# Dividing the loads of an attention and expert kernel into pieces, issued at two marks of every step

## The chip, the cores and the metric

The kernel runs on one core of one Trainium2 chip. The metric is device time in microseconds (us) of one execution. An execution is measured several times, and the median is compared. The profile comes from one execution that the hardware profiler recorded, with a time of its own.

Engines in the text: TensorE (PE in profile lines; PEld is its weight loads), VectorE (DVE), ScalarE (ACT), GpSimd (POOL) and SyncE (SP), which only issues transfers. GpSimd issues transfers as well, and those that change the number type go through it. Every engine works through its own instructions in order, and waits on semaphores for others.

## The reference

Sliding-window attention with a few sink positions, and then a sparse layer that only 128 tokens of each batch pass through. Shapes are 4 batches, 8 heads, 768 positions, 64 values to a head; the window is 128 wide and the first 4 positions are sinks.

```python
scores = 1 / sqrt(D) * q @ k.T                    # per batch and head, 768 x 768
keep = (pos[None, :] < 4) | ((rel >= 0) & (rel < 128))      # rel = query - key
a = softmax(where(keep, scores, -1e9))
x = (a @ v) laid out as [batch, position, 8 * 64]
s = x @ w_gate                                    # one score per token
top = the 128 tokens of each batch with the largest s
out = x
out[top] = x[top] + sigmoid(s[top]) * (relu(x[top] @ w1) @ w2)
```

w1 is 512 x 1024 and w2 is 1024 x 512, all inputs are float32.

## The kernel before

The attention is cut into 24 steps. A step is (b, g, jp): batch b, group g of four heads (0 or 1), and a pair jp of query blocks of 128 positions (0, 1, 2). The loop at line 455 runs over them with n from 0 to 23; s = 3g + jp counts the six steps of a batch. The order of instructions on each engine is the order in which the code is written, since the scheduling is manual.

Within a step, TensorE computes the scores of the next step (`scores`, line 214), ScalarE takes their exponentials (line 255) into `PT`, and TensorE multiplies those by the values (`values`, line 259, once for t = 0 and once for t = 1, two heads each). VectorE then divides by the row sums (lines 275 and 276) into X. Query and key come in as 128-position rows with several heads beside each other, and `transposes` (line 187) turns them: K of the coming group after the values of jp = 0, Q before the values of jp = 1. VectorE and ScalarE copy the results out of PSUM.

Half a block of queries (64 rows) sees one whole block of 128 keys, one half block and the sinks. So each matmul over values reads one of three tiles: `vb` holds the values as loaded, a whole block of 128 keys; `vE` holds the lower 64 rows of a block and below them the sink values; `vF` holds sink values and the upper 64 rows. `half_values` (line 115) copies those halves out of `vb`, on GpSimd after the first steps, in pieces of two blocks for all four heads; `sink_values` (line 111) loads the sink rows with two small transfers on SP. There are two `vb` buffers, each for a batch with all eight heads, and two of `vE` and `vF`, one for each group.

Loads are issued like this:

- K and Q, with a change from float32 to bfloat16, by GpSimd (`load_qk`, line 84). One load brings four heads, 384 KB as the profile counts it. The loads of a group of batch b + 1 are issued in the first two steps of the same group of batch b.
- The first group's K and Q in eight loads (`load_qk_first`, line 92), and then K and Q of the second group directly behind them.
- Values by SP: the first six blocks one by one (line 107), the second group of batch 0 in one load (line 165 and above), and then two heads at a time (`load_v`, line 102), at s = 0, 1, 2 and 4.
- w1 and w2 by GpSimd in two loads each, at s = 0 and 2, and at s = 3 and 5 of batch 1 (lines 512 to 517).
- The finished rows are stored by SP, two blocks in one transfer, at the end of each step of g = 1 (`finish_rows`, line 289).

SP's and GpSimd's transfers each use eight semaphores in turn, so a transfer also waits for the eighth before it on its queue.

The sparse layer of a batch runs beside the attention of the next batch (`m` in the loop: `spread`, `count`, `columns`, `ranks`, `choose`, `index`, `gather`) and of the one after that (`mm`: `pick`, `up`, `down`, `scatter`). The last batch's sparse layer follows the loop (lines 547 to 570).

Two small functions in the opening, `first_values` (line 158) and `late_loads` (line 163), set buffers to constants and issue loads; `late_consts` and `late_consts2` make index tables.

## Time and profile before

| what | us |
|---|---|
| median of 3 runs | 153.49 (151.84 to 153.93) |
| the profiled execution | 154.2 |
| its span, first to last instruction | 152.4 |
| mean granted TensorE clock | 0.939 of full speed |

The busy time of each engine over the span, with its number of instructions, is this:

```profile
PE 114.7 (75%) x2888; PEld 96.2 (63%) x2888; DVE 99.3 (65%) x306; ACT 69.8 (46%) x92; POOL 61.6 (40%) x99
```

The transfers are these (queue, packets, MB, and the time of the packets as a share of 16 transfer engines over the span). Queue 0 holds what GpSimd issues, queue 1 what SP issues:

```profile
q0 software_dynamic: 7200, 10.49, 38.7%
q1 hardware_dynamic: 28868, 13.28, 33.9%
```

And this is the granted TensorE clock in 40 slices of the span, in tenths:

```profile
PEclk9998699969999997899599999999999999999985
```

Shares of busy time are means over the whole span, and they hide that the loop ends at some 131 us and that a tail of some 20 us without bulk loads follows. The last value loads are issued at 94.72 us, and the last step's division ends at 131.6 us. Idle time of one engine costs nothing unless another waits for it, so the waits have to be read beside the busy time. A wait is put down to what came last by the profile; "issue" is a wait for nothing that the profile shows.

### The profile page before, as it was taken

To read this page: it belongs to the slowest core of one execution; us is meant where nothing else is said; L and a number is where in the kernel's file an instruction comes from. 1 tells how busy PE (TensorE), PEld (TensorE's weight loads), DVE (VectorE), ACT (ScalarE), POOL (GpSimd) and SP (SyncE) were. 2 spreads that over 40 slices of the span, in tenths; PEclk is the share of its full clock that TensorE was granted. 3 is DMA by queue.
4 is the path that set the end of the run, shared out by engine and by line. 5 is a ranking of instruction groups with operands and counts; after the bars stand their busy time and mean duration, and the time that the engine had idled before them with its cause. 6 is when DMAs were issued, how large, how long until landed. Compare 5 with 4: busy or idle time off the path is not lost. (4 is left out here: it accounts for less than half of the span.)

```text
span 152.4 us, 6554 instructions
## 1 busy us (share of the span) xinstructions
PE 114.7 (75%) x2888; PEld 96.2 (63%) x2888; DVE 99.3 (65%) x306; ACT 69.8 (46%) x92; POOL 61.6 (40%) x99
## 2 busy tenths in 40 slices
PE   6846996389599575983986959799897988886700
PEld 2325886289489366873876848669696975746600
DVE  5726787239569971693675945967799958956220
ACT  3084454525568341552564608517755673250200
POOL 7947879085097000960594018414610021102220
PEclk9998699969999997899599999999999999999985
DMA  2799999999979999699999983973300044411201
GB/s 37 107 168 173 252 247 228 235 141 217 263 244 141 207 206 223 162 174 240 321 191 201 205 187 28 269 268 133 94 4 4 4 164 187 156 55 69 73 2 69
DMA packets 36098, 24.19 MB, mean 159 GB/s; under 512 B 25829, under 2 KB 31845, under 8 KB 36069
## 3 DMA queue, kind: packets, MB, share of 16 engines
q0 software_dynamic: 7200, 10.49, 38.7%
q1 hardware_dynamic: 28868, 13.28, 33.9%
q8 instruction: 23, 0.38, 1.0%
q14 instruction: 7, 0.05, 0.1%
HBM read 24.41 MB, written 7.34 MB: 208 GB/s over the span
## 5 line engine op out<-in xcount | busy, mean ns | idle before, releaser
L255 ACT ACTIVATE pt<-sc 128x1024 f32<-128x1024 f32 (+1 forms) x48 | 43.5, 951 | 25.8 <-PE sc L250 25.5
L270 PE MATMUL xg<-vb,pt 128*64 128x65 f32 x704 | 50.7, 233 | 5.8 <-issue 5.8
L270 PE MATMUL xg<-vE,pt 128*64 128x65 f32 x384 | 47.0, 235 | 8.5 <-issue 4.3
L270 PEld LDWEIGHTS xg<-vb,pt 128*64 128x64 f32 x704 | 46.1, 146 | 6.3 <-issue 6.3
L270 PEld LDWEIGHTS xg<-vE,pt 128*64 128x64 f32 x384 | 37.7, 147 | 11.9 <-issue 10.0
L270 PE MATMUL xg<-vF,pt 128*64 128x65 f32 x320 | 41.2, 229 | 0.0
L270 PEld LDWEIGHTS xg<-vF,pt 128*64 128x64 f32 x320 | 33.1, 145 | 0.0
L117 POOL COPY vE<-vb 64x512 f32<-64x512 f32 (+1 forms) x27 | 15.7, 587 | 36.1 <-DMA vb<-in_v_dram 29.6
L275 DVE RECIPROCAL rz<-xg 128x4 f32<-128x4 f32 x48 | 8.6, 179 | 28.6 <-PE xg L270 28.3
L276 DVE TENSOR_TENSOR x<-xg,rz 128x256 f32<-128x256 f32 x48 | 20.4, 424 | 1.7
L118 POOL COPY vF<-vb 64x512 f32<-64x512 f32 x21 | 14.2, 677 | 15.2 <-PE sc L250 6.4
L226 PE MATMUL sc<-QT,KT 64*64 64x192 bf16 (+2 forms) x384 | 17.1, 251 | 3.3 <-issue 1.9
L286 DVE CUSTOM_DVE_ANT_0 junk<-x,wgb 128x512 f32<-128x512 f32 (+1 forms) x30 | 18.8, 661 | 0.3
L336 DVE TENSOR_SCALAR_CACHE_REDUCE G<-sbc,scol 128x512 bf16<-128x512 f32 (+5 forms) x26 | 15.4, 637 | 0.4 <-ACT sbc L318 0.3
L232 PE MATMUL sc<-band,ident_b 64*64 64x256 bf16 x192 | 14.2, 282 | 0.0
L226 PEld LDWEIGHTS <-KT 64*64 64x64 bf16 x384 | 8.1, 110 | 6.8 <-issue 3.6
L245 PE MATMUL sc<-QT,ksk 64*64 64x128 bf16 (+1 forms) x96 | 10.5, 214 | 1.3 <-issue 1.3
L434 POOL DMA_INDIRECT out_dram<-yo,idx x4 | 4.1, 1018 | 18.0 <-DVE yo L430 17.2
L207 ACT COPY KT<-trp 128x768 bf16<-128x768 bf16 x7 | 5.7, 809 | 12.2 <-PE trp L197 12.2
L250 PE MATMUL sc<-QT,ksk 64*64 64x128 bf16 x96 | 10.9, 225 | 0.0
L375 POOL DMA_INDIRECT xe<-out_dram,idx x4 | 4.2, 1054 | 15.8 <-issue 12.2
L197 PE MATMUL trp<-ident_b,kb 128*64 128x128 bf16 x192 | 8.7, 241 | 1.1 <-DMA kb<-in_k_dram 1.0
(96 smaller groups left out, 185.7 us busy)
## 6 DMA issues: line engine op xcount, KB each, us to landing
out_dram<-x SPq DMA_DIRECT2D x12, 512.0 KB
vb<-in_v_dram SPq DMA_DIRECT2D x12, 384.0 KB
kb<-in_k_dram POOLq DMA_DIRECT2D x7, 384.0 KB, 7.8
qb<-in_q_dram POOLq DMA_DIRECT2D x7, 384.0 KB, 9.4
w_sb<-in_moe_w_dram POOLq DMA_DIRECT2D x4, 512.0 KB, 7.8
vb<-in_v_dram SPq DMA_DIRECT2D x6, 128.0 KB
vb<-in_v_dram SPq DMA_DIRECT2D x1, 768.0 KB
kb<-in_k_dram POOLq DMA_DIRECT2D x4, 96.0 KB, 3.5
```

The costliest lines, as they stand in the source:

```text
L117: e.tensor_copy(out=vE[g][0:64, c0:c1, :, 0:D], in_=src[0:64])
L118: f.tensor_copy(out=vF[g][64:128, c0:c1, :, 0:D], in_=src[64:128])
L197: PE.transpose(out=trp[64 * l:64 * l + 64, i, :], in_=src[:, l, half * (CT // 2) + i, :], identity=ident_b[:])
L226: PE.matmul(out=sc[e][64 * h:64 * h + 64, l, i, 64 * h:64 * h + n], lhsT=kt[r, e, q0:q0 + 64], rhs=qt[r, e, q0:q0 + n], start=(i == 0), st ...
L232: PE.matmul(out=sc[e][64 * h:64 * h + 64, l, :, :].rearrange("p k (a x n) -> p k a x n", a=2, x=2)[:, :, :, h, :], lhsT=ident_b[r, r], rhs ...
L245: PE.matmul(out=sc[e][0:64, l, 0:n, 192:256], lhsT=ksk[g][r, e, :], rhs=(qt[r, e, q0 - 64:q0 - 64 + 256].rearrange("p (k c) -> p k c", k=2 ...
L250: PE.matmul(out=sc[e][64:128, l, 0:2, 0:64], lhsT=ksk[g][r, e, :], rhs=qs, start=False, stop=True, skip_group_check=True)
L255: ACTE.activation(out=pt[:, :, :, :].rearrange("p l k c -> p l (k c)")[:, :, 0:n], in_=sc[e][:, :, :, :].rearrange("p l k c -> p l (k c)") ...
L270: PE.matmul(out=xg[64 * m:64 * m + 64, i, l, :], lhsT=PT[(b, g, kc // 2, t)][:, l, kc % 2, off:off + 64], rhs=val, start=first[m], stop=(i ...
L276: DVE.tensor_tensor(out=X[b][:, js[0]:js[0] + 2, 256 * g:256 * g + 256].rearrange("p j (l e d) -> p j l e d", l=2, e=2)[:, :, :, t, :], in ...
L286: DVE.tensor_tensor_reduce(out=junk[:, c0:c1], in0=X[b][:, j, c0:c1], in1=wgb[:, c0:c1], scale=1.0, scalar=0.0, op0=ALU.mult, op1=ALU.add, ...
L336: DVE.tensor_scalar(out=self.G[c][:, lo:z], in0=self.sbc[:, lo:z], scalar1=SCOL[self.b][:, c:c + 1], scalar2=0.0, op0=ALU.is_gt, op1=ALU.a ...
```

## The change

`load_qk` now loads one pair of heads of K or Q, `load_v` one head, and `load_w` a quarter of w1 or w2. Before most of these loads, `gate` writes one element of the destination on VectorE. The load overwrites that element, so it has to wait until VectorE has come to the gate. The gates are at two marks of a step: after the division for t = 0, and at the step's end.

The value buffers hold four heads each and there are three of them, used in turn by the groups; the row pitch of a block in them (`VS`) is 128 elements and not 96. `half_values` now copies one head with all its blocks, and leaves out the vF copy of the last block, which no matmul reads. The second group's Q and values of batch 0 are loaded from step 0's first mark on. Values of the coming groups are loaded from jp = 2 of the group two before to jp = 0 of the group before, K and Q over the three steps of the group two before. The eight weight pieces go out at the ends of steps 5 to 8 and 11 to 14. Rows are stored one block at a time by `store_rows`, ahead of the sink loads.

```diff
@@ -23,7 +23,7 @@
 FF = 1024
 NSINK = 4
 VW = D + 1
-VS = 96
+VS = 128
 CT = 12
 
 
@@ -61,7 +61,7 @@
     def const(shape, dt, name):
         return cp.tile(shape, dt, name=name, tag=name)
 
-    vb = [const([128, H, NB, VS], FP32, f"vb{i}") for i in range(2)]
+    vb = [const([128, 4, NB, VS], FP32, f"vb{i}") for i in range(3)]
     vE = [const([128, NB, 4, VW], FP32, f"vE{i}") for i in range(2)]
     vF = [const([128, NB, 4, VW], FP32, f"vF{i}") for i in range(2)]
     vsk = const([NSINK, 2 * B, 4, VW], FP32, "vsk")
@@ -81,13 +81,19 @@
 
     QK, KT, QT, PT, X, SCOL = {}, {}, {}, {}, {}, {}
 
-    def load_qk(b, g, ts=(0, 1)):
-        for t in ts:
-            dst = stg.tile([128, 2, CT, D], BF16, name=("kb", "qb")[t], tag=("kb", "qb")[t])
-            QK.setdefault((b, g), [None, None])[t] = dst
-            POOL.dma_start(
-                out=dst[:, :, :, :].rearrange("p l c d -> p l (c d)"),
-                in_=(k, q)[t][b, 4 * g:4 * g + 4, :, :].rearrange("(l e) (p c) d -> (e p) l (c d)", e=2, c=CT))
+    def gate(ap):
+        DVE.memset(ap, 0.0)
+
+    def load_qk(b, g, t, l, gated=True):
+        if l == 0:
+            QK.setdefault((b, g), [None, None])[t] = stg.tile([128, 2, CT, D], BF16, name=("kb", "qb")[t],
+                                                              tag=("kb", "qb")[t])
+        dst = QK[(b, g)][t]
+        if gated:
+            gate(dst[0:1, l, 0, 0:1])
+        h = 4 * g + 2 * l
+        POOL.dma_start(out=dst[:, l, :, :].rearrange("p c d -> p (c d)"),
+                       in_=(k, q)[t][b, h:h + 2, :, :].rearrange("e (p c) d -> (e p) (c d)", c=CT))
 
     def load_qk_first(half):
         if half == 0:
@@ -99,9 +105,10 @@
                     in_=src[0, 0:4, 384 * half:384 * half + 384, :].rearrange(
                         "(l e) (p c) d -> e p l (c d)", e=2, c=6)[e])
 
-    def load_v(b, h0, h1):
-        SP.dma_start(out=vb[b % 2][:, h0:h1, :, 0:D].rearrange("p h c d -> p (h c) d"),
-                     in_=v[b, h0:h1, :, :].rearrange("h (c p) d -> p (h c) d", p=128))
+    def load_v(b, g, hh):
+        buf = vb[(2 * b + g) % 3]
+        gate(buf[0:1, hh, 0, 0:1])
+        SP.dma_start(out=buf[:, hh, :, 0:D], in_=v[b, 4 * g + hh, :, :].rearrange("(c p) d -> p c d", p=128))
 
     def load_v_block(c):
         SP.dma_start(out=vb[0][:, 0:4, c, 0:D],
@@ -112,10 +119,21 @@
         SP.dma_start(out=vE[g][64:64 + NSINK, :, :, :].rearrange("s c h o -> s c (h o)"), in_=src)
         SP.dma_start(out=vF[g][0:NSINK, :, :, :].rearrange("s c h o -> s c (h o)"), in_=src)
 
-    def half_values(b, g, c0, c1, e, f):
-        src = vb[b % 2][:, 4 * g:4 * g + 4, c0:c1, 0:D].rearrange("p h c d -> p c h d")
-        e.tensor_copy(out=vE[g][0:64, c0:c1, :, 0:D], in_=src[0:64])
-        f.tensor_copy(out=vF[g][64:128, c0:c1, :, 0:D], in_=src[64:128])
+    def half_values(b, g, c0, c1, h0, h1, e, f):
+        src = vb[(2 * b + g) % 3][:, h0:h1, c0:c1, 0:D].rearrange("p h c d -> p c h d")
+        e.tensor_copy(out=vE[g][0:64, c0:c1, h0:h1, 0:D], in_=src[0:64])
+        if c0 < NB - 1:
+            c1 = min(c1, NB - 1)
+            f.tensor_copy(out=vF[g][64:128, c0:c1, h0:h1, 0:D], in_=src[64:128, 0:c1 - c0])
+
+    def load_w(i):
+        if i < 4:
+            gate(w1_sb[0:1, i, 0:1])
+            POOL.dma_start(out=w1_sb[:, i, :], in_=moe_w1.rearrange("(dc p) f -> p dc f", p=128)[:, i, :])
+        else:
+            r = slice(2 * i - 8, 2 * i - 6)
+            gate(w2_sb[0:1, 2 * i - 8, 0:1])
+            POOL.dma_start(out=w2_sb[:, r, :], in_=moe_w2.rearrange("(fc p) d -> p fc d", p=128)[:, r, :])
 
     def fill(times):
         f = w_ps.tile([128, 512], FP32, name="fill", tag="w")
@@ -135,7 +153,8 @@
         POOL.affine_select(out=r[:, 1, :], in_=r[:, 1, :], compare_op=ALU.is_ge, fill=-1e9, base=-1,
                            pattern=[[-1, 64]], channel_multiplier=1)
     load_qk_first(1)
-    load_qk(0, 1)
+    for l in range(2):
+        load_qk(0, 1, 0, l, gated=False)
     DVE.memset(vsk[:, :, :, D:VW], 1.0)
     SP.dma_start(out=vsk[:, :, :, 0:D].rearrange("s (b g) h d -> s (b g h) d", b=B),
                  in_=v[:, :, 0:NSINK, :].rearrange("b h s d -> s (b h) d"))
@@ -161,7 +180,6 @@
             load_v_block(c)
 
     def late_loads():
-        load_v(0, 4, 8)
         SP.dma_start(out=wgb[:], in_=moe_w_gate.partition_broadcast(128))
         POOL.memset(vE[1][64:128, :, :, :], 0.0)
         POOL.memset(vF[1][0:64, :, :, :], 0.0)
@@ -169,6 +187,7 @@
         POOL.memset(vF[1][64:128, :, :, D:VW], 1.0)
         POOL.memset(ksk[1][:], 0.0)
         DVE.memset(vb[1][:, :, :, D:VW], 1.0)
+        DVE.memset(vb[2][:, :, :, D:VW], 1.0)
         DVE.memset(ones_b[:], 1.0)
 
     iotas = []
@@ -262,7 +281,7 @@
         for i, j in enumerate(js):
             for l in range(2):
                 hh = 2 * l + t
-                whole = vb[b % 2][:, 4 * g + hh, :, 0:VW]
+                whole = vb[(2 * b + g) % 3][:, hh, :, 0:VW]
                 terms = [(0, j, 0, vE[g][:, j, hh, :]), (1, j, 64, whole[:, j, :])]
                 if j > 0:
                     terms += [(0, j - 1, 128, whole[:, j - 1, :]), (1, j - 1, 192, vF[g][:, j - 1, hh, :])]
@@ -286,11 +305,13 @@
             DVE.tensor_tensor_reduce(out=junk[:, c0:c1], in0=X[b][:, j, c0:c1], in1=wgb[:, c0:c1], scale=1.0,
                                      scalar=0.0, op0=ALU.mult, op1=ALU.add, accum_out=acc[:, j:j + 1])
 
+    def store_rows(b, js):
+        for j in js:
+            SP.dma_start(out=out[b, j * 128:(j + 1) * 128, :], in_=X[b][:, j, :])
+
     def finish_rows(b, js):
         if js[0] == 0:
             SCOL[b] = sp.tile([128, NB], FP32, name="scol", tag="scol")
-        SP.dma_start(out=out[b, js[0] * 128:(js[-1] + 1) * 128, :].rearrange("(j p) d -> p j d", p=128),
-                     in_=X[b][:, js[0]:js[-1] + 1, :])
         if b < B - 1:
             dots(b, js, 0, DM, SCOL[b])
             return
@@ -448,7 +469,7 @@
     for t in range(2):
         transposes(0, 0, t, (1,))
     for c in range(2):
-        half_values(0, 0, c, c + 1, POOL, DVE)
+        half_values(0, 0, c, c + 1, 0, 4, POOL, DVE)
     late_loads()
 
     moe = {}
@@ -457,6 +478,7 @@
         js = [2 * jp, 2 * jp + 1]
         last = b == B - 1
         nxt = (b, 1) if g == 0 else (b + 1, 0)
+        far = (b + 1, g)
         m, mm = moe.get(b - 1), moe.get(b - 2)
         if n + 1 < len(steps):
             nb, ng, njp = steps[n + 1]
@@ -478,43 +500,52 @@
                 if m and s == 0:
                     m.spread(0, NB)
                     m.gates_exp()
+                if nxt[0] < B:
+                    if n == 0:
+                        for l in range(2):
+                            load_qk(0, 1, 1, l)
+                        load_v(*nxt, 0)
+                        load_v(*nxt, 1)
+                    if jp == 0:
+                        load_v(*nxt, 2)
+                if far[0] < B:
+                    if jp > 0:
+                        load_qk(*far, jp - 1, 1)
+                    if jp == 2:
+                        load_v(*far, 0)
         if last and s == 4:
             moe[b].count((0, 1))
         if m and s == 3:
             m.index()
         if nxt[0] < B and jp == 0:
             transposes(nxt[0], nxt[1], 0)
-        if b + 1 < B:
-            if s == 0:
-                X[b + 1] = xp.tile([128, NB, DM], FP32, name="x", tag="x")
-            if s in (0, 1, 2, 4):
-                h = 2 * (0, 1, 2, 0, 3)[s]
-                load_v(b + 1, h, h + 2)
-            if s in (0, 1):
-                load_qk(b + 1, 0, (s,))
-            if s in (3, 4):
-                load_qk(b + 1, 1, (s - 3,))
+        if b + 1 < B and s == 0:
+            X[b + 1] = xp.tile([128, NB, DM], FP32, name="x", tag="x")
+        if g == 1:
+            store_rows(b, js)
+        if nxt[0] < B:
+            if jp == 0:
+                sink_values(*nxt)
+                load_v(*nxt, 3)
+        if far[0] < B:
+            if jp < 2:
+                load_qk(*far, jp, 0)
+            else:
+                load_v(*far, 1)
+        if 5 <= n < 9:
+            load_w(n - 5)
+        if 11 <= n < 15:
+            load_w(n - 7)
+        if n < 2:
+            for c in range(2 * n + 2, 2 * n + 4):
+                half_values(0, 0, c, c + 1, 0, 4, POOL, DVE)
+        if nxt[0] < B:
+            for hh in ((), (0, 1), (2, 3))[jp] if n < 3 else ((0,), (1, 2), (3,))[jp]:
+                half_values(*nxt, 0, NB, hh, hh + 1, POOL, POOL)
         if n == 0:
             late_consts()
         if n == 1:
             late_consts2()
-        if nxt[0] < B:
-            if jp == 0:
-                sink_values(*nxt)
-            if n > 2:
-                half_values(*nxt, 2 * jp, 2 * jp + 2, POOL, POOL)
-            elif n == 2:
-                for c in (0, 2, 4):
-                    half_values(*nxt, c, c + 2, POOL, POOL)
-        if n < 2:
-            for c in range(2 * n + 2, 2 * n + 4):
-                half_values(0, 0, c, c + 1, POOL, DVE)
-        if b == 1 and s in (0, 2):
-            r = slice(s, s + 2)
-            POOL.dma_start(out=w1_sb[:, r, :], in_=moe_w1.rearrange("(dc p) f -> p dc f", p=128)[:, r, :])
-        if b == 1 and s in (3, 5):
-            r = slice(2 * (s - 3), 2 * (s - 3) + 4)
-            POOL.dma_start(out=w2_sb[:, r, :], in_=moe_w2.rearrange("(fc p) d -> p fc d", p=128)[:, r, :])
         if last and g == 0:
             dots(b, js, 0, 256, PART)
         if g == 1:
```

## The prediction

> **What bounds the kernel now.** I read the page first, then the waits of TensorE, then the timeline around its longest idle times, then tables by stretches of time. Two rows of the page's 40 slices (3.81 us each) set the question:
>
> ```profile
> PE   6846996389599575983986959799897988886700
> DMA  2799999999979999699999983973300044411201
> ```
>
> While the DMA row stands at 9 (8 to 87 us), TensorE falls to 5 and 3 again and again; once the DMA row is at 3 and 0 (103 us on), TensorE stays at 8 and 9. ScalarE and GpSimd are far from full. The waits of TensorE from 14 to 108 us (engine, line, what it waited for, us in all, times, longest) are these:
>
> ```profile
> PE xg L270 <- issue: 10.1, 6, 2.4
> PE xg L270 <- DMA vE<-vsk: 4.2, 2, 2.6
> PE sc L226 <- issue: 1.9, 2, 1.6
> PE sc L245 <- issue: 1.3, 1, 1.3
> ```
>
> "issue" means that nothing the profile shows was waited for. Where such a wait falls is the clue (the timeline of TensorE: start, us, line, operation, count, idle time before):
>
> ```profile
> 50.50 0.24 PE L226 MATMUL sc<-QT,KT 64*64 64x192 bf16 x1
> 52.36 0.36 PE L226 MATMUL sc<-QT,KT 64*64 64x192 bf16 x7 [1.62 <-issue]
> ```
>
> One of eight equal score matmuls runs, 1.62 us pass, and the other seven follow. All eight read the same KT and QT and write one tile, so no data can be missing. Long waits end at 24.08, 31.06, 42.01, 52.36, 58.79, 71.09, 83.20, 89.51 and 99.24 us; they took 1.32, 1.41, 1.88, 1.62, 2.65, 2.42, 1.30, 1.84 and 1.25 us, 15.7 us together. I counted TensorE's instructions between neighbours in a table by stretches (from, to, length, then busy us and count of PE, PEld, DVE, ACT, POOL, then the granted clock, the DMA share and GB/s):
>
> ```profile
> 30.00:40.50 10.50, 9.07 (x255) 8.31 (x255) 7.37 (x20) 4.96 (x6) 5.32 (x8) 0.84 1.01 200
> 51.00:57.00 6.00, 3.78 (x126) 3.33 (x125) 4.98 (x19) 2.91 (x4) 0.00 (x0) 1.00 1.15 207
> 57.00:70.00 13.00, 9.39 (x255) 8.65 (x255) 7.68 (x21) 5.82 (x7) 6.00 (x8) 0.87 0.95 191
> ```
>
> Matmuls plus weight loads are 510, 251, 510; the other five stretches give 259, 509, 507, 254, 508. That is 256 or twice 256 every time. The page has a queue for instructions:
>
> ```profile
> q8 instruction: 23, 0.38, 1.0%
> ```
>
> That is 23 packets of 16.5 KB; the 2 x 2888 matmuls and weight loads of the whole run are 22.6 times 256. So I read these nine waits as TensorE's program arriving late, behind the bulk loads: between 108 and 152 us, with a mean DMA share of 0.20, the list of TensorE's waits names no "issue". The 2.65 us at 58.79 is named a DMA of sink values, but falls on the same count and its issue lies 14 us back. Only the wait at 28.66 (1.53 us, same name) stands off the count; it is a sink load behind a 768 KB and a 384 KB value load on SP.
>
> The Trainium skill ("Runtime: NRT & Kernel Launch", "Instruction fetch mechanics") says that blocks of 256 instructions are fetched while the present one runs and are mostly hidden, with room for 2,048 on TensorE. By that rule the nine waits would not be fetches, and this change would have only the 1.53 us to win, and the sum below would come to 156.6 us. The row with seven of eight matmuls speaks against the rule here.
>
> **The change, part by part.** The sum is made against the profiled execution: 154.2 us, of which the span is 152.4. The median of the three runs is 153.49, so 0.7 comes off at the end. The bytes stay the same.
>
> *Smaller pieces, spread out.* A group's K or Q load of 384 KB becomes two of 192, a value load of 384 KB becomes two of one head (192 KB), a weight load of 512 KB two of 256. The issue lines of the page give the length of what a fetch stands behind (count, KB, median us to landing):
>
> ```profile
> kb<-in_k_dram POOLq DMA_DIRECT2D x7, 384.0 KB, 7.8
> qb<-in_q_dram POOLq DMA_DIRECT2D x7, 384.0 KB, 9.4
> kb<-in_k_dram POOLq DMA_DIRECT2D x4, 96.0 KB, 3.5
> qb<-in_q_dram POOLq DMA_DIRECT2D x4, 96.0 KB, 4.1
> ```
>
> On a straight line between these, 192 KB lands in about 5 to 6 us, some 3 us sooner; the longest wait is 2.65, so all 15.7 us could go. Against that stands the ceiling: from 14.3 to 107.9 us the DMA share is 0.98 of 93.6 us, 91.7 us of work, and the highest share held over 7 us is 1.17 (22.6 to 30.0). That work needs 91.7/1.17 = 78.4 us, so at most 15.2 us can be saved, and a loop that gets faster loads the queues as before. Bounds 0 and 15.2; I take two thirds of 15.7, **-10.5**.
>
> *The sink wait.* Three value pieces (576 KB) instead of the loads named above now precede that sink load: **-1.5**, bounds 0 and 1.5.
>
> *The clock.* After such waits the granted clock is 0.78 (32.4 to 37.8 us), 0.78 (54.9 to 61.7) and 0.66 (72.5 to 77.3): 5.4x0.22 + 6.8x0.22 + 4.8x0.34 = 4.3 us at the most. In the first of these VectorE is busy 4.69 of 5.4 us and would hold the step anyway. **-1.5**, bounds 0 and 4.3.
>
> *The start.* Q of group (0,1) was issued at 8.59 us; now it waits for a mark after the first normalising (VectorE, 16.51 + 0.42 = 16.9), two issues of 0.72 follow, and it lands 3.5 to 6 us later, at 22 to 24. Its transposes stand ahead of step 1's values on TensorE, which now reaches them near 19.5: 2 to 4.5 us lost. In return the first K and Q halves, for which TensorE waits 0.46 and 1.91 us at 9.72 and 12.15, no longer share the engines with it or with 768 KB of values. Bounds -0.4 and +4.5; **+2.0**.
>
> *The gates.* 62 one-element memsets on VectorE; the nearest rows are 65 and 72 ns (one-partition memsets, lines 153 and 159): 4.3 us of VectorE. What queues behind each is the normalising that frees TensorE's xg. A gate's own wait (earlier readers and loads of that buffer) is over steps before. VectorE is near full only in the steps that copy transposes (4.69 of 5.4, 4.61 of 4.7, 5.17 of 5.7 us), a third of all: **+1.4**, bounds 0 and 4.3.
>
> *GpSimd.* 18 more load issues at 0.72 = 13 us, copies 28 pairs of 384 and 320 columns instead of 21 pairs of 512. By the uncontended rows (0.39 us for 256 columns, 0.60 for 512) a pair is 0.49 + 0.44, 26 us against 25.5. GpSimd goes from 61.6 to about 75 busy us, well under the span. Each issue now waits for VectorE's mark, and the value copies, gathers and scatters stand behind it. This bites where a weight piece comes before head 3's copies at the end of a group (steps 5, 8, 11, 14): normalising 0.65, gate 0.1, issue 0.72, copies 0.93 and some 0.2 of signals make 2.6 us, while TensorE comes to head 3 after the next scores and half the values, 0.95 + 0.95. 4 x 0.6 = 2.4 at most; **+1.2**.
>
> *SP.* 27 more issues of about 0.4 us, on a queue that mostly waits. A store or sink load behind a gated load now waits for a mark as well; sinks are still issued over two steps before use. Nothing added, and up to 1.5 us per group if a sink is late. Leaving out the last block's unused vF copy and the new row pitch of the value tile: nothing; both lie on GpSimd or in transfers, and are in the pairs counted above.
>
> Sum: 154.2 - 10.5 - 1.5 - 1.5 + 2.0 + 1.4 + 1.2 = 145.3, less 0.7: **144.6 us**.
>
> Shares above 1 in the stretches shown say that several loads are in flight at once, so the number of loads (45 more) costs their issue and no more. A rule against all this is in the Trainium skill, "DMA: Bandwidth & Descriptors", "Bandwidth" and "Anatomy of one DMA": transfers should be 1 MiB or more, and each has about 2 us of fixed cost. By it, as an estimate, 45 x 2 = 90 us if they ran one by one, for some 235 us.
>
> **The rivals.** *The waits stay (no change).* If a fetch stands behind all that is queued and not behind one load, the same bytes at a share near 1 delay it as before. For it: the shares of stretches with waits are 0.94 to 1.17 whatever was loading. With half the 15.7 us kept: 154.2 - 7.8 + 4.6 = 151.0, less 0.7 = 150.3; with all kept, 158.8 - 0.7 = 158. I put its centre at 152.
>
> *The marks make Q late (slower).* Q's last piece is issued half-way through a group's third step and is transposed before the values of the next group's second step: 1.5 steps, 6.6 us at 4.4 us a step. Landing above that stops TensorE once per group. At 9.4 us (the median of the large Q loads) it costs 2.8 x 7 = 19.6 us: 164 us. It decides from a landing of about 7.9, where 1.3 x 7 eats the gain of 8.9. Against it: the small loads land in 4.1, at shares of about 0.8 to 1.08, however.
>
> *The pieces are not pieces:* no; the changed program issues each load by itself.
>
> **How the numbers follow.** About 2% (3.1 us) is what a measurement of this kernel can tell from no change. The forecast has 0.70, the first rival 0.17, the late Q 0.13. The forecast's best case is the ceiling, 154.2 - 15.2 - 0.7 = 138.3. The range runs from 139 to 156, with 0.06 below and 0.13 above. Faster 0.70, same 0.17, slower 0.13.
>
> **What would show it.** Right: waits for "issue" on TensorE from 14 to 108 us fall from 13 to 3 or 5 us; steps 3 to 17 (26.4 to 104.5 us now, 5.2 us each) take 4.4 to 4.7; the DMA share there goes above 1.05; a new wait for Q near 20 us. Wrong: issue waits still on multiples of 256 and near 10 us (first rival); waits of TensorE for qb in most groups (second); GpSimd's copies in front of TensorE's waits for vE (my 1.2 too small).

## The result, and the profile after

The changed kernel is slower: 161.69 us (160.02 to 161.78, four runs) against 153.71 (151.84 to 154.72, four runs) of the kernel before beside it. The ratio is 1.054, with a 95% interval of 1.041 to 1.066. The profiled execution took 161.74 us, its span 159.8, and the mean granted clock was 0.901 (0.939 before). Here and below a median is over all executions, and a ratio compares the faster executions of a kernel (within 1.5% of its fastest) with those of the kernel before in the same session.

First the rows of the page's 40 slices (now 4.0 us each):

```profile
PE   6846906699978694998149996799499887895900
POOL 7922870393773672078315590465336010202220
PEclk9995675899999999699956999999879999999995
DMA  3899496279899999789975799989950025331110
```

TensorE stands still in the sixth slice (20 to 24 us), and the clock in the slices after it is 0.5 to 0.8. The DMA row now has gaps at 16 to 20 and at 24 to 32 us, where before it stood at 9: loads are held back just before and just after TensorE's wait, and while it waits (20 to 24) the row is at 9. The waits of TensorE from 14 to 115 us (line, what it waited for, us in all, times, longest) say what took the place of the old ones:

```profile
PE xg L289 <- POOL vF L127: 5.6, 3, 3.3
PE trp L216 <- DMA qb<-in_q_dram: 5.1, 2, 4.8
PE xg L289 <- issue: 4.6, 3, 2.5
PE xg L289 <- POOL vE L124: 3.6, 3, 1.9
PE trp L216 <- issue: 1.5, 1, 1.5
PE sc L245 <- issue: 1.3, 1, 1.3
PE sc L251 <- issue: 0.8, 1, 0.8
```

The four "issue" rows make 8.2 us. Before they made 13.3, and 15.9 with the 2.65 us that the list names a DMA of sinks. The sink row is gone. New are 5.1 us for Q, once, and 9.2 us for the two copies that GpSimd makes.

Where this falls is seen when a fixed event of every step is compared: the first division of step n (VectorE's reciprocal, from its timeline), in us.

| step n | before | after | after minus before |
|---|---|---|---|
| 2 | 25.46 | 33.30 | +7.84 |
| 11 | 71.58 | 71.60 | +0.02 |
| 13 | 81.60 | 88.34 | +6.74 |
| 15 | 92.91 | 96.11 | +3.20 |
| 19 | 113.42 | 120.85 | +7.43 |
| 23 | 129.75 | 137.44 | +7.69 |

So the start loses 7.8 us, steps 2 to 11 win 7.8 (somewhat over half of the gain that was expected), and from there to step 19 another 7.4 are lost. From the first division of step 12 to that of step 13 the change takes 7.55 us longer (88.34 - 74.64 against 81.60 - 75.45), of which 3.5 come back by step 15, and at step 18 2.8 us longer (120.85 - 111.02 against 113.42 - 106.40). In both GpSimd has issued a gather shortly before. Little changes after that.

**The start.** GpSimd's timeline (start, us, line, operation, count, idle time before):

```profile
15.90 1.39 POOL L184 MEMSET vE<- 64x1560 f32 x1
17.35 1.39 POOL L185 MEMSET vF<- 64x1560 f32 x1
...
19.55 1.07 POOL L95 DMA_DIRECT2D qb<-in_q_dram  x2 [0.28 <-DVE x L295]
```

The mark itself was set at 17.97 us. The Q loads of group (0,1) still had to stand behind some 3.3 us of GpSimd's own constants (`late_loads`), which ran to 19.26, 1.3 us past the mark. TensorE's timeline shows the bill:

```profile
24.96 0.28 PE L216 MATMUL trp<-ident_b,qb 128*64 128x128 bf16 x1 [4.81 <-DMA qb<-in_q_dram]
25.52 1.46 PE L216 MATMUL trp<-ident_b,qb 128*64 128x128 bf16 x23 [0.28 <-DMA qb<-in_q_dram]
```

And then the clock (a table by stretches: from, to, length, busy us and count of PE, PEld, DVE, ACT, POOL, granted clock, DMA share, GB/s):

```profile
25.50:29.70 4.20, 4.18 (x87) 4.20 (x87) 1.73 (x5) 0.81 (x1) 0.00 (x0) 0.57 0.22 46
```

At a clock of 0.57 the values of step 1 take longer than they would at full speed, so the wait costs more than its own length. Of the 7.8 us, 1.1 come from step 0 (its first division at 17.39 instead of 16.30; in the other versions it lies between 15.82 and 17.65). From there to step 2, TensorE waits 6.5 us (5.1 for Q, 1.4 for a copy) instead of 1.6. The other 1.8 fit the clock, 4.2 us at 0.57, but no run shows that part by itself. The DMA share is 0.22 there and GpSimd idle, since its next load waits for a mark as well:

```profile
29.71 0.54 POOL L95 DMA_DIRECT2D kb<-in_k_dram  x1 [6.47 <-DVE kb L85]
```

**The gathers.** GpSimd's timeline around the first gather, after:

```profile
74.45 1.19 POOL L396 DMA_INDIRECT xe<-out_dram,idx  x1 [0.28 <-POOL vF L127]
77.01 0.50 POOL L124 COPY vE<-vb 64x384 f32<-64x384 f32 x1
81.19 0.45 POOL L127 COPY vF<-vb 64x320 f32<-64x320 f32 x1 [3.68 <-DMA xe<-out_dram,idx]
```

and TensorE behind it:

```profile
77.56 0.27 PE L289 MATMUL xg<-vE,pt 128*64 128x65 f32 x1 [1.94 <-POOL vE L124]
...
81.69 0.37 PE L289 MATMUL xg<-vF,pt 128*64 128x65 f32 x1 [3.33 <-POOL vF L127]
```

The vF copy that follows a gather on GpSimd waits in this program until the gather has landed, and this copy is of head 3 of the group that TensorE has already begun. In the kernel before the same dependence is there, and TensorE's list names no copy. The rows are the first gather there; the last one, from GpSimd's list of waits, shows the dependence at the second:

```profile
65.72 1.20 POOL L375 DMA_INDIRECT xe<-out_dram,idx  x1 [0.28 <-POOL vF L118]
66.96 0.60 POOL L117 COPY vE<-vb 64x512 f32<-64x512 f32 x1
73.94 1.02 POOL L118 COPY vF<-vb 64x512 f32<-64x512 f32 x1 [6.38 <-PE sc L250]
...
POOL vF L118 <- DMA xe<-out_dram,idx: 5.0, 1, 5.0
```

Before, the gather goes out 1.1 us ahead of the first division of step 10 (66.85), after the change 5.4 us behind it (69.08). Of the 9.2 us for copies, 7.6 lie in steps 12 and 18. And the copies by pairs of blocks were needed one step after another, those by heads are all needed in the group's first step. (The version without marks, below, has the copies by heads too, and TensorE waits for none of them.)

### The profile page after: what moved, and what is told of

It reads as the page before. It is cut to its first block, busy times and chain, and to the rows that moved or that the text cites. A ratio compares the mean times of both kernels' runs of the same rounds, so it can differ in the third digit from the quotient of the medians.

```text
span 159.8 us, 6749 instructions
## 1 busy us (share of the span) xinstructions
PE 118.5 (74%) x2885; PEld 99.1 (62%) x2888; DVE 95.1 (60%) x368; ACT 69.8 (44%) x92; POOL 70.2 (44%) x131
## 5 line engine op out<-in xcount | busy, mean ns | idle before, releaser
L289 PE MATMUL xg<-vb,pt 128*64 128x65 f32 x704 | 50.0, 231 | 0.0
L95 POOL DMA_DIRECT2D kb<-in_k_dram x14 | 7.6, 548 | 32.7 <-PE trp L216 14.2
L124 POOL COPY vE<-vb 64x384 f32<-64x384 f32 (+1 forms) x34 | 17.7, 527 | 7.3 <-DMA vb<-in_v_dram 5.9
L127 POOL COPY vF<-vb 64x320 f32<-64x320 f32 x28 | 13.5, 484 | 11.0 <-DMA xe<-out_dram,idx 7.1
L305 DVE CUSTOM_DVE_ANT_0 junk<-x,wgb 128x512 f32<-128x512 f32 (+1 forms) x30 | 17.1, 606 | 0.3
L251 PE MATMUL sc<-band,ident_b 64*64 64x256 bf16 x192 | 14.7, 285 | 0.8 <-issue 0.8
L216 PE MATMUL trp<-ident_b,qb 128*64 128x128 bf16 x192 | 9.0, 248 | 7.6 <-DMA qb<-in_q_dram 7.5
L226 ACT COPY KT<-trp 128x768 bf16<-128x768 bf16 x7 | 5.7, 809 | 19.2 <-PE trp L216 19.2
L216 PEld LDWEIGHTS <-qb 128*64 128x64 bf16 x192 | 7.4, 127 | 9.3 <-issue 8.6
L216 PE MATMUL trp<-ident_b,kb 128*64 128x128 bf16 x192 | 9.9, 259 | 2.1 <-issue 1.5
L455 POOL DMA_INDIRECT out_dram<-yo,idx x4 | 4.0, 1007 | 16.2 <-DVE yo L451 15.9
```

The source lines that it names most:

```text
L95: POOL.dma_start(out=dst[:, l, :, :].rearrange("p c d -> p (c d)"), in_=(k, q)[t][b, h:h + 2, :, :].rearrange("e (p c) d -> (e p) (c d)", ...
L124: e.tensor_copy(out=vE[g][0:64, c0:c1, h0:h1, 0:D], in_=src[0:64])
L127: f.tensor_copy(out=vF[g][64:128, c0:c1, h0:h1, 0:D], in_=src[64:128, 0:c1 - c0])
L216: PE.transpose(out=trp[64 * l:64 * l + 64, i, :], in_=src[:, l, half * (CT // 2) + i, :], identity=ident_b[:])
L251: PE.matmul(out=sc[e][64 * h:64 * h + 64, l, :, :].rearrange("p k (a x n) -> p k a x n", a=2, x=2)[:, :, :, h, :], lhsT=ident_b[r, r], rhs ...
L289: PE.matmul(out=xg[64 * m:64 * m + 64, i, l, :], lhsT=PT[(b, g, kc // 2, t)][:, l, kc % 2, off:off + 64], rhs=val, start=first[m], stop=(i ...
```

## The experiments

Each edit is to the changed kernel unless it says otherwise. "Issue" sums below are from the list of TensorE's waits from 14 to 115 us, each from a single profile. In the order in which they stand here, the first four come from one session, the next three from a second, the next four from a third and the last from a fourth. The kernel before had medians of 154.13, 153.16, 152.76 and 153.62 us in them, so a difference of medians across sessions is uncertain by a us or more, and the ratios, each to the kernel before of the same session, are given too.

**Q of (0,1) back in the opening.**

```diff
-    for l in range(2):
-        load_qk(0, 1, 0, l, gated=False)
+    for t in range(2):
+        for l in range(2):
+            load_qk(0, 1, t, l, gated=False)
...
                     if n == 0:
-                        for l in range(2):
-                            load_qk(0, 1, 1, l)
                         load_v(*nxt, 0)
```

> The changed kernel with one part undone: Q of group (0,1) is issued without a gate, directly behind K of that group, as before the change. Theory A (the opening's late Q costs what step 1 lost): TensorE's wait for qb near 20 us (4.81 us) is gone, step 1's first division comes at about 22 to 24 us instead of 28.75, and the time falls by 4 to 6 us to about 156 to 157.5. Rival (the wait moves to the next late thing, as the DMA engines are free from 26 to 31 us anyway): step 3 comes as late as before, and the time stays within 1.5 us of 161.7.

Measured: 153.49 us (152.25 to 156.47, ten runs), ratio to before 0.996 [0.991, 1.001]. Two load issues moved back, without their marks, take 8.2 us off, nearly the whole loss, and more than was expected. The rest of the list stays:

```profile
PE xg L290 <- POOL vF L127: 3.8, 2, 2.8
PE xg L290 <- issue: 3.7, 6, 1.2
PE xg L290 <- POOL vE L124: 2.5, 3, 1.5
```

**The copies of heads 1 to 3 one step earlier, ahead of the gather.**

```diff
-            for hh in ((), (0, 1), (2, 3))[jp] if n < 3 else ((0,), (1, 2), (3,))[jp]:
+            for hh in ((), (0, 1), (2, 3))[jp] if n < 3 else ((0,), (1, 2, 3), ())[jp]:
```

> The changed kernel with the copies of heads 1, 2 and 3 all at the end of a group's second step (before the gather), none at the end of the third. Theory B (head 3's copies stand behind the gather on GpSimd, and its vF copy waits for the gather's landing): TensorE's waits for vE and vF (9.2 us in the changed kernel) fall to under 3, steps 12 and 18 no longer lose 4.9 and 2.5 us, and the time falls by 5 to 8 us to 154 to 157. Rival (GpSimd is simply late with everything): the waits for vE and vF stay over 6 us and the time stays within 1.5 us of 161.7.

> Both edits together. If A and B are separate losses, they add: 161.7 - 5 - 6.5, about 149 to 152, faster than the kernel before. If one hides the other: 154 to 157.

Measured: alone 162.22 us (158.51 to 164.17), ratio 1.056 [1.045, 1.067]; together with the early Q 155.13 (149.39 to 158.18), not told apart from before and inside the range named for losses of which one hides the other. Alone the waits for the copies fell to 1.7 us, but the wait moved. In the first of the two:

```profile
PE xt L414 <- DMA xe<-out_dram,idx: 6.6, 2, 4.5
PE trp L216 <- DMA qb<-in_q_dram: 5.6, 3, 3.0
PE xg L289 <- issue: 5.3, 4, 1.7
PE xg L289 <- POOL vE L124: 1.7, 2, 1.4
```

TensorE's transposes of the gathered rows (`xt`) now wait for the gather itself. So not the order of copy and gather is the fault: GpSimd comes to both too late.

**The kernel before with the same pieces** (K, Q, value, weight loads and stores cut as in the change; no marks, no third buffer, the old places):

```diff
-            POOL.dma_start(
-                out=dst[:, :, :, :].rearrange("p l c d -> p l (c d)"),
-                in_=(k, q)[t][b, 4 * g:4 * g + 4, :, :].rearrange("(l e) (p c) d -> (e p) l (c d)", e=2, c=CT))
+            for l in range(2):
+                h = 4 * g + 2 * l
+                POOL.dma_start(out=dst[:, l, :, :].rearrange("p c d -> p (c d)"),
+                               in_=(k, q)[t][b, h:h + 2, :, :].rearrange("e (p c) d -> (e p) (c d)", c=CT))
```

> The kernel before with every load and store divided into the same pieces, all issued at the places of before, without gates, buffers by batch as before. Theory C (a fetch of TensorE's instructions stands behind what is queued altogether, so only spreading helps): issue waits on multiples of 256 instructions stay at 12 to 16 us in all, time within 2 us of 153.5. Rival (it stands behind the one load in front of it, as the prediction had it): they fall to under 8 us and the time falls to 145 to 149.

Measured: 156.01 us (150.76 to 159.25), not told apart from before. The waits that the pieces should have shortened are still there:

```profile
PE xg L271 <- issue: 8.8, 5, 2.7
PE sc L227 <- issue: 2.7, 1, 2.7
```

All "issue" rows make 11.8 us (13.3 before). The size of a load is at most a small part of what these waits depend on.

**The gather earlier** (early Q, and the gather given out before the values of a batch's fifth step instead of at its end):

```diff
+        if m and s == 4:
+            m.gather()
         for t in range(2):
             values(b, g, js, t)
...
-            elif s == 4:
-                m.gather()
```

> The changed kernel with Q of group (0,1) issued early (as in e1_q_early) and each gather issued at the start of step s = 4, ahead of that step's loads and copies on GpSimd. Theory B (head 3's copies and then TensorE stand behind the gather's landing, because pacing GpSimd by the marks has put the gather some 6 us later in the steps): the waits for vF at steps 12 and 18 (2.8 and 1.0 us) go, no wait of TensorE for the gather takes their place, and the time is 3 to 5 us under e1_q_early, 148.5 to 150.5. Rival (another late thing is close behind): 151.5 to 154.

Measured: 148.87 us (147.63 to 149.56), ratio 0.981 [0.971, 0.992], less than both kernels. Against the early Q alone it is 4.6 us less in the medians, 1.5% (2.2 us) by the ratios. TensorE's list no longer has vF or xe; of the copies there remains

```profile
PE xg L290 <- POOL vE L124: 5.2, 4, 3.0
```

of which 2.95 us end at 69.58 us, where a copy still stands behind one that waits for the gather, and the rest lies in the first steps.

**No marks** (early Q; all memsets of `gate` are left out, pieces, places and buffers stay):

```diff
     def gate(ap):
-        DVE.memset(ap, 0.0)
+        pass
```

> e1_q_early without the 62 one-element memsets, so that every load goes out as soon as its queue and its buffer allow; pieces, buffers and order of issue as in the changed kernel. Theory D (the marks are what spaces the loads, and so lets TensorE's instructions through): on-count issue waits rise from some 9 us back to 13 to 16, time 154 to 158. Rival (the gates mostly delay): the time falls to 149 to 152.

Measured: 147.19 us (146.35 to 148.67), ratio 0.975 [0.960, 0.990], below both ranges named. Against the same with marks it is 6.3 us less in the medians, 2.1% (3.2 us) by the ratios. TensorE's list has no copy and no gather, but the "issue" waits are back:

```profile
PE xg L290 <- issue: 7.0, 6, 2.2
PE trp L217 <- issue: 3.5, 2, 3.2
```

and GpSimd reaches the gather 1.4 us after the first division of step 10 (60.32 us):

```profile
61.69 1.05 POOL L397 DMA_INDIRECT xe<-out_dram,idx  x1 [0.28 <-POOL vF L127]
64.85 0.50 POOL L124 COPY vE<-vb 64x384 f32<-64x384 f32 x1 [0.78 <-PE xg L290]
66.51 0.46 POOL L127 COPY vF<-vb 64x320 f32<-64x320 f32 x1 [1.16 <-DMA xe<-out_dram,idx]
```

The marks thus go with two things: shorter "issue" waits, and a GpSimd that is held up. The second is the larger here; whether the first is their doing is taken up below.

**The program shifted** (the kernel before, its 11 opening matmuls of 512 columns cut into 44 of 128, so that 33 matmuls and 33 weight loads come on top at the start):

```diff
-    fill(11)
+    fill(11, 4)
```

> The kernel before with the eleven opening filler matmuls of 512 columns cut into 44 of 128 columns: the same multiplications, 66 more TensorE instructions ahead of all else. Theory (the issue waits are block boundaries of TensorE's program): the waits fall at the same counts of instructions (193 over a multiple of 256), that is, 66 instructions earlier in the program than before. Rival (they belong to a place in the program, some data): they fall at 66 instructions more in the count, 3 over a multiple of 256. Time within 3 us of before.

Measured: 155.51 us in a single execution. Counting from the start into one of the "issue" waits, before (a table by stretches):

```profile
0.00:23.50 23.50, 17.30 (x348) 12.22 (x349) 15.60 (x40) 11.02 (x14) 17.50 (x38) 0.93 0.95 166
```

and in the shifted kernel:

```profile
0.00:22.50 22.50, 17.62 (x348) 15.21 (x349) 13.68 (x37) 10.04 (x13) 17.06 (x37) 0.85 0.95 167
```

Both stretches end inside a wait (22.76 to 24.08 us before, 22.04 to 22.75 here), after 348 matmuls and 349 weight loads. With 66 instructions on top, the wait stands at the same count and thus 66 instructions earlier in the work: before between two score matmuls of one step, now among the matmuls over values. The next one comes after 948 matmuls and weight loads before and 952 here, and the last long one after 3,997 in both. With TensorE's other instructions counted too, all nine long waits of before and the ten of over 0.5 us here stand at 193 over a multiple of 256 (one at 191). The waits belong to the count of TensorE's instructions, not to an operation.

The traces also hold the instruction packets themselves (queue 8). One runs from 50.03 to 50.91 us in the kernel before, and the wait that the prediction shows ends at 52.36. All these waits, the nine and the ten, end 1.3 to 1.6 us after such a packet has landed. In every version the packets from 14 to 100 us take about 1 us (medians 0.94 to 1.02). Those behind the nine waits start when TensorE has gone through 180 or more of the 256 instructions of a block; from 110 to 125 us, without bulk loads, they start within some 50. So the waits are for the program, and a fetch that is late does not last longer: it starts late.

**Which half of the marks, and the place of Q.** Four versions without all or part of the marks, with Q of (0,1) in the opening unless said.

Marks on the value loads alone:

```diff
-        if gated:
-            gate(dst[0:1, l, 0, 0:1])
...
-            gate(w1_sb[0:1, i, 0:1])
...
-            gate(w2_sb[0:1, 2 * i - 8, 0:1])
```

Marks on K, Q and weight loads alone:

```diff
-        gate(buf[0:1, hh, 0, 0:1])
```

> Marks on the value loads alone (SP's queue); K, Q and weight loads go out on GpSimd without any; Q of (0,1) in the opening. Theory (the marks cost because GpSimd, which also makes the value copies and starts the gathers, stands still at them): all of the 6.3 us between 153.5 and 147.2 stay won, 145 to 148, with no wait of TensorE for vF above 1 us. Rival (any mark delays loads): 150 to 153, with values late and so vE and vF.

> The other half: marks on K, Q and weight loads alone, value loads go out on SP without any; Q of (0,1) in the opening. Theory (GpSimd standing still at marks is the cost): 152 to 154, as with all marks, with TensorE waiting 3 to 7 us for vE and vF. Rival (the marks on SP are the cost): 146 to 149.

Measured, in one session: marks on SP's loads alone 148.90 us (146.76 to 149.74), ratio 0.990 [0.980, 1.000]; on GpSimd's loads alone 154.30 (151.64 to 155.73), not told apart from before. Their ranges do not overlap, and the medians are 5.4 us apart. In the second, TensorE's list is that of the change again without the start:

```profile
PE xg L289 <- POOL vF L126: 6.4, 2, 3.2
PE xg L289 <- issue: 5.0, 3, 3.1
PE xg L289 <- POOL vE L123: 4.3, 4, 1.9
```

GpSimd's place shows it most directly. Each entry is the time at which the gather is issued less the time of the first division of step 10 (first gather) or 16 (second):

| kernel | first gather | second |
|---|---|---|
| before | 65.72 - 66.85 = -1.1 | 95.28 - 98.39 = -3.1 |
| the change | 74.45 - 69.08 = +5.4 | 108.39 - 102.56 = +5.8 |
| early Q, all marks | 67.24 - 62.09 = +5.2 | 99.92 - 93.59 = +6.3 |
| marks on GpSimd's loads alone | 67.45 - 62.29 = +5.2 | 99.45 - 94.19 = +5.3 |
| marks on SP's loads alone | 63.66 - 62.86 = +0.8 | 91.96 - 91.16 = +0.8 |
| early Q, early gather, all marks | 62.77 - 62.43 = +0.3 | 91.42 - 91.08 = +0.3 |
| no marks | 61.69 - 60.32 = +1.4 | 89.04 - 91.47 = -2.4 |

> The changed kernel without its marks, Q of (0,1) left where the change put it, in step 0. Splits the loss at the start into place and mark. Theory (the place does it: two Q loads stand behind 3.3 us of GpSimd's own memsets, and without a mark they are issued at about 18 instead of 19.6): TensorE still waits 3 us or more for qb near 20 us, and the time is 147.2 + 4 to 6 = 151 to 153. Rival (the mark does it): the wait for qb is under 1 us, 147 to 148.

Measured, no marks but Q of (0,1) in step 0: 151.42 us (148.78 to 153.65), ratio 0.995 [0.984, 1.007]. Its Q is issued at 16.88 us (19.55 with the mark), still behind the constants, and TensorE waits

```profile
20.99 0.24 PE L216 MATMUL trp<-ident_b,qb 128*64 128x128 bf16 x1 [1.47 <-DMA qb<-in_q_dram]
22.30 1.42 PE L216 MATMUL trp<-ident_b,qb 128*64 128x128 bf16 x23 [1.07 <-DMA qb<-in_q_dram]
```

2.5 us instead of 5.1. The wait there is under the 3 us named, the time within the 151 to 153 named. In the traces the first division of step 2 comes at 28.53 us here and at 24.68 with the early Q and no marks; with all marks it comes at 33.30 (the change) and 26.61 (early Q). By these numbers 3.9 of 6.7 us lost at the start are the place, the rest the mark. The medians are less sure: 4.2 us for the place against the version without marks of another session, 2.3 against the one that follows.

> The pieces, order and buffers of the change, Q of (0,1) in the opening, no mark on any load, and the gather given out before the values of each batch's fifth step. In the version without marks no wait of TensorE for vE, vF or xe is left, since GpSimd reaches the gather in time by itself. Theory (what the early gather won with marks, 153.5 to 148.9, was only the delay that the marks had put on GpSimd): nothing more is won, 146 to 148. Rival (the gather stands late in its own right): a further 2 to 4 us, 143 to 145.

Measured, no marks, early Q and the gather earlier: 149.15 us (147.06 to 151.82), ratio 0.982 [0.963, 1.001]. Nothing is won beside 147.19 without the move (the median is above the 146 to 148 named, the ranges overlap). The early gather pays only where the marks have made GpSimd late.

**The copies ahead of the marks** (all marks, early Q, early gather; at the end of a step `half_values` now precedes the marked loads):

```diff
+        if nxt[0] < B:
+            for hh in ((), (0, 1), (2, 3))[jp] if n < 3 else ((0,), (1, 2), (3,))[jp]:
+                half_values(*nxt, 0, NB, hh, hh + 1, POOL, POOL)
         if far[0] < B:
             if jp < 2:
                 load_qk(*far, jp, 0)
...
-        if nxt[0] < B:
-            for hh in ((), (0, 1), (2, 3))[jp] if n < 3 else ((0,), (1, 2), (3,))[jp]:
-                half_values(*nxt, 0, NB, hh, hh + 1, POOL, POOL)
```

(The copies of the first two steps were moved in the same way.)

> The version with all marks, Q of (0,1) in the opening and the early gather (148.87), and at the end of each step the value copies now stand ahead of that step's marked K, Q and weight loads on GpSimd, so that the copies no longer wait for the marks. Theory (the marks shorten the program-fetch waits to 6 to 9 us, and what they cost is that GpSimd stands at them with copies queued behind): TensorE's 5.2 us of waits for vE fall to 2 or less, the waits on the instruction count stay at 6 to 9 us, 144.5 to 147. Rival (the copies wait for their own value loads and now hold the K and Q loads back): waits for qb grow from 3.8 us to 6 or more, 149 to 152.

Measured: 150.77 us (148.02 to 155.04), ratio 0.977 [0.962, 0.993]. The waits for vE fell from 5.2 to 2.0 us as the theory said, but Q is late instead, and the time is the rival's. TensorE's waits over the whole span:

```profile
PE trp L217 <- DMA qb<-in_q_dram: 6.7, 6, 1.8
PE xg L290 <- issue: 4.0, 5, 1.5
PE xg L290 <- POOL vE L124: 2.0, 2, 1.1
```

GpSimd in its order has either copies behind marks or loads behind copies.

**All "issue" sums together**, 14 to 115 us:

| no marks on GpSimd's loads | us | marks on GpSimd's loads | us |
|---|---|---|---|
| before | 13.3 | the change | 8.2 |
| before, in pieces | 11.8 | early Q | 7.3 |
| before, shifted | 19.2 | copies earlier | 7.2 |
| no marks | 11.3 | both | 4.9 |
| no marks, early gather | 11.7 | early Q, early gather | 5.4 |
| no marks, late Q | 11.8 | marks on GpSimd's loads alone | 7.3 |
| marks on SP's loads alone | 12.2 | copies ahead of the marks | 6.4 |

The lowest on the left is above the highest on the right. That does not show that spaced loads bring the program sooner. In the same stretch TensorE waits another 9.0 to 15.6 us for copies, gathers, Q and the like in the versions on the right, and 2.8 to 6.0 in those on the left, and a late instruction block need not cost anything while TensorE stands for something else: in the change, the packets of 20.90 and 76.27 us landed while it waited for Q and for a copy. Between the first divisions of steps 2 and 11 those other waits make at most 2.4 us in the versions below, and there the marks make little difference (us, from one profile each):

| kernel | steps 2 to 11 | "issue" in it | steps 11 to 23 |
|---|---|---|---|
| before | 46.1 | 7.3 (10.0 with the misnamed one) | 58.2 |
| before, in pieces | 44.7 | 8.6 | 59.5 |
| the change | 38.3 | 5.7 | 65.8 |
| early Q | 39.8 | 5.4 | 62.3 |
| marks on GpSimd's loads alone | 39.0 | 5.7 | 65.3 |
| marks on SP's loads alone | 39.1 | 7.2 | 56.8 |
| no marks | 39.6 | 6.3 | 57.9 |

Of the 7.8 us that the change wins in steps 2 to 11, 6.5 are won without any mark, and the pieces at the old places win only 1.5. The other 5 go with what the version without marks has and the one in pieces has not: the new places and order of the loads, the three value buffers and the copies by heads. No run takes these apart. The last column shows what the marks on GpSimd's loads cost.

## Why the prediction was wrong

The forecast was 144.6 us and faster; the time is 161.69 and slower, outside the range of 139 to 156. Term by term, against the sum of the prediction:

- **Smaller pieces, -10.5.** The nine waits were read rightly as TensorE's program: they stay on the instruction count when the program is shifted, and each ends just after an instruction packet. The step that failed is that a fetch waits as long as one load lands, so that half the load means a shorter wait. Cut into the same pieces, the kernel before keeps 11.8 of 13.3 us, and the packets do not last longer, they start late. In the change 8.2 us are left, 5.1 less (7.7 with the misnamed one), and part of the difference may be hidden behind its new waits. In steps 2 to 11, where little hides them, they fall from 10.0 to 5.7 us, and to 6.3 without any mark: so what shortens them is for the most part neither the pieces nor the marks but something in the new places, order and buffers. The rival "the waits stay" was half right, for the pieces.
- **The sink wait, -1.5.** Right: the row is gone.
- **The clock, -1.5.** Wrong in sign: 0.901 instead of 0.939. New waits took the place of the old ones, and the clock after the longest was 0.57 for 4.2 us.
- **The start, +2.0 (bounds -0.4 to +4.5).** The mechanism was right, a wait for Q before step 1's values. The size was 7.8 us, of which 1.1 had gone by in step 0. The sum took the mark at 16.9 and the issue straight behind it; the mark came at 17.97, GpSimd had 3.3 us of constants ahead of the load and issued it at 19.55, and it landed at 25 and not at 22 to 24. The second part is the low clock after the wait. Undoing it alone gives 8.2 us back.
- **The gates, +1.4.** They were priced as VectorE's instructions, 62 of some 0.07 us (59 ns each in the trace). That price is not seen: with marks on SP's loads alone, 148.9 us, against 147.2 with none, whose runs overlap. Their real price is what stands behind them on GpSimd.
- **GpSimd, +1.2 (bound 2.4).** This is the term that failed most after the start. The prediction said that value copies, gathers and scatters stand behind each marked issue, and then priced only the copies of head 3 behind weight loads. The gathers were named and given no price. They come 5.4 us after a step's first division instead of 1.1 us before it, and the next copy waits for their landing: TensorE waits 9.2 us for copies, and steps 11 to 23 take 65.8 us instead of 58.2. With marks on SP's loads alone they take 56.8, and with marks on GpSimd's loads alone 65.3; these two are 5.4 us apart in their medians, in one session. Moving only the gather gives 2.2 us by the ratios, 4.6 by the medians. The prediction's last sign of being wrong, GpSimd's copies in front of TensorE's waits for vE, is what came.
- **SP, 0.** Right.
- **The rival "late Q once per group"** happened once and at the place where Q was moved, not in every group: in the change both waits for qb from 14 to 115 us are for this one load. (In other versions Q is late in other groups: 6.1 us in the one with early Q and earlier copies, 4.9 in the one with the copies ahead of the marks.)

The three terms that had to be added, +2.0, +1.4 and +1.2, were in truth about 7.8, 0 and some 7.7 (steps 11 to 23); the gain was about 7.8 (steps 2 to 11) and not 13.5. Since GpSimd's lateness was entered as four small overlaps, no rival had it as its one mechanism, and the range did not reach the time. Of the signs for being right only the new wait for Q came: steps 3 to 17 took 5.1 us each and not 4.4 to 4.7, and the DMA share there was 0.97 and not above 1.05.

What stays open: which part of the new order shortens the waits for the program, and why the fetches start late. Some 2 of the 7.8 us that steps 2 to 11 win are not put down to a wait either (5.7 us of "issue" waits instead of 10.0 there, and 1.5 of sinks). And the five versions from 147 to 151 us are not told apart from each other. The change without its marks and with the early Q, 147.19 us, has the lowest median, 0.975 [0.960, 0.990] of before; it and the version with marks, early Q and early gather (0.981 [0.971, 0.992]) are faster than the kernel before, but whether by 2% is not settled.

## What to carry to other kernels

Before a load is given a mark to wait for, list what its issuing engine does next in order, indirect transfers too, and price each of them by when its reader comes, not only the mark's own instruction. A load that is moved later is issued when its engine is free and not when its mark is set; look for the constants, copies and issues ahead of it. When a change does several things (here smaller loads, spaced loads and a new order), price and test them apart: here the gain came without the spacing, and the spacing brought the cost. When one kind of wait shrinks while another grows, compare a stretch in which the other is absent before crediting the change.

## What the runs showed of the hardware that was not expected

- TensorE's waits for its program stood after the same count of its instructions, 348 matmuls and 349 weight loads for the one shown, with 66 instructions added at the start or without. They made 11.3 to 13.3 us from 14 to 115 us in six kernels whose GpSimd loads were not spaced (19.2 in the shifted one). The instruction packets took about 1 us, late or not; behind the waits they started late in a block. That agrees with blocks of 256 instructions as the Trainium skill has it ("Runtime: NRT & Kernel Launch", "Instruction fetch mechanics"); that crossing such a block is mostly hidden does not agree with single waits of 2.4 us (before) and 4.4 us (shifted) here.
- One wait of 4.8 us of TensorE was followed by a clock of 0.57 for the next 4.2 us, though TensorE was busy for 4.18 of them; it had been 0.65 from 16 to 20 us, ahead of that wait.
